# Fused attention and feed-forward kernel: the first two feed-forward groups in an attention PSUM tile, ScalarE ahead of VectorE on the transposes, k's sums by TensorE, and a new order at both ends of batch 1

## The chip, the core and the metric

The kernel runs on one core of one Trainium2 chip. The metric is the device time in microseconds (us) of one execution. Five engines take part, each with its own instruction stream that runs in order: TensorE (PE in the profile, its weight loads PEld), VectorE (DVE), ScalarE (ACT), GpSimd (POOL) and SyncE (SP, which here only issues DMAs). They wait for each other by semaphores.

## What is computed

Two stages, one after the other, over 8 batches of 576 tokens with 8 heads of 64. The attention of a head is the sum of two parts: a *global* one on q, k and v averaged over groups of four tokens (144 positions, repeated four times at the end), and a *local* one in which a token sees only tokens less than four away.

```python
q_d = q.reshape(B, H, Sd, factor, D).mean(axis=3)       # the same for k and v; factor 4
out_up = np.repeat(sm_attn(q_d, k_d, v_d), factor, axis=2)
mask = np.abs(pos[:, None] - pos[None, :]) < factor
attn = softmax(np.where(mask, scale * q @ k.T, -1e9))
x = (out_up + attn @ v), as [B*S, H*D]                   # 4608 x 512
h = x @ w_in                                             # 512 x 2048
g = np.where(h > 0, h, np.exp(np.minimum(h, 0)) - 1)
out = g @ w_out                                          # 2048 x 512
```

## The kernel before

**Attention.** Work goes by pairs of heads: four pairs a batch, named (batch, pair). For each pair the kernel transposes q and k on TensorE into the PSUM tiles `tq` and `tk`, copies them to SBUF as `qt` and `kt`, multiplies them to scores `sc` (six local blocks of 102x96, L362, and the global 72x144 products, L377), takes exponentials on ScalarE (`pex` local, `dex` global), masks the local ones on VectorE (`mex`), sums denominators with matmuls, takes a reciprocal on VectorE, spreads the reciprocals over 64 partitions each (`rcb`), multiplies with v to `lg`, scales `lg` on VectorE to `gn` and `ln`, and adds the two on GpSimd into `xt`, the input of the feed-forward part. The group averages are kept as sums: `kd` for k, the tail of `qt` for q, `vd` for v. There are three forms of the beginning of a pair. Batch 0 uses `early_transposes` and takes the sums of q and k on VectorE (`sums`, L252) from the finished copies. Batch 1 uses `early_transposes` too, but lets TensorE make the sums into columns of the same PSUM tile (12 more matmuls against the constant `EI`), and VectorE copies them out (L295); its `vd` goes through a corner of `tq` and `tk` as well (L281, L285). Batches 2 to 7 use `transposes`.

**Feed-forward.** Nine blocks of 512 tokens. `mm1(t, fc)` makes one of 16 groups of 128 hidden channels: four 128x128 by 128x512 matmuls into a bank `hp` (L592), an exponential on ScalarE (`e`, L608), two VectorE instructions (L609, L612) that finish the activation in `gt`. `mm2(t, i)` is a quarter of an output tile of 128 tokens: four matmuls into `op` (L623); every fourth ends with a copy on ScalarE (`os`) and a DMA on SP. For block 0, groups 0 and 1 are split: `mm1_begin` does the first three of the four matmuls, which need head pairs 0 to 2 only, and `mm1` does the last one (L600) once pair 3's part of `xt` is there.

**PSUM.** There are eight banks. The tag `two` is a ring of two tiles of two banks each; `tq`, `tk`, the two `sc`, the two `rb` of `spread_pe` and `lg` take turns in it, so that each waits until the tile before it in its slot has been read. The other four banks belong in batch 0 to `rb` and `lg` (pool `pse`), and from `swap_pools` on to the tags `hp` and `misc`, two banks each (pool `psm`); `swap_pools` needs batch 0's last reads to be over.

**Order.** The order of all work is written out by hand. Batch 0 is the list `order`, with extras per pair in `early` and `late`; everything after it is put at a time by `at` and sorted. A step that stands at 13.5 comes after `mm1` of group 13. `slots` holds the times of a batch's transposes and scores, `d0` that of the denominators, `o0` those of the outputs, `mm2_at` those of the output quarters. In batch 0 and early in batch 1 matmuls on zeros (`warm`, `keep_busy`, L152) stand where TensorE would have nothing to do.

**Queues.** v of all batches, and q and k from batch 2 on, come through SP as fp32 and are cast on GpSimd (`cast`). q and k of batches 0 and 1 (`load_qk`, two pairs a call but for the first) and the weights `WI`, `WO` (`load_weights`, eight pieces) are issued by GpSimd and cast on the way. So GpSimd's stream mixes DMA issues, casts and the additions into `xt`.

Of the kernel before, what the change touches and what calls it, by code (L numbers as in the profile page):

```python
# [11 lines left out]
AB = mybir.AluOpType  # L12
AF = mybir.ActivationFunctionType
# [85 lines left out]
def kernel(  # L99
# [156 lines left out]
    def early_transposes(b, j):  # L256
# [10 lines left out]
        for t, x16 in ((tq, q16), (tk, k16)):  # L267
# [3 lines left out]
            if b >= NEARLY:  # L271
                for c in range(NB):
# [4 lines left out]
                         skip_group_check=True)  # L277
            if b >= NEARLY:
                g = 0 if t is tq else 1
# [5 lines left out]
                nc.vector.tensor_copy(out=vd[:, g, :], in_=t[0:KG, 0, HB : HB + 128])  # L285
# [6 lines left out]
            if b < NEARLY:  # L292
                sums(y, x)
            else:
                nc.vector.tensor_copy(  # L295
                    out=_free(y[:, 0:1], [[3, 48], [1, 3]]),
                    in_=_free(t[:, 1, HB : HB + 1], [[1, 48], [48, 3]]),
                )
        stT[(b, j)] = (qt, kt, kd, vd)
# [286 lines left out]
    def mm1_begin(t, fc, n):  # L586
# [3 lines left out]
        hp = hps[fc] = bank("misc" if t == 0 and fc < 12 and fc % 4 >= 2 else "hp", "hp")  # L590
        for dc in range(n):
            nc.tensor.matmul(  # L592
                hp[:], WI[:, dc, 128 * fc : 128 * fc + 128], xts[t][:, dc, :],
# [3 lines left out]
    def mm1(t, fc):  # L597
        if t == 0 and fc < 2:
            hp = hps[fc]
            nc.tensor.matmul(  # L600
                hp[:], WI[:, DMC - 1, 128 * fc : 128 * fc + 128], xts[t][:, DMC - 1, :],
                start=False, stop=True,
            )
        else:
# [3 lines left out]
        nc.scalar.activation(out=e[:], in_=hp[:], func=AF.Exp)  # L608
# [4 lines left out]
            out=gts[t][:, fc, :], in0=hp[:], scalar=0.0, op0=AB.max, in1=e[:], op1=AB.add  # L613
# [24 lines left out]
    def at(time, fn, *args):  # L638
# [3 lines left out]
    open_pool("pse")  # L642
    order = [
        (load_consts, 0, 3), (load_qk, 0, (0,)), (load, 0, 0), (load_qk, 0, (1,)), (load_qk, 1),
        (load, 0, 1), (load, 0, 2), (warm, 9), (early_transposes, 0, 0), (load_consts, 3, 4),
        (cast, 0, 0), (load, 0, 3), (warm, 5), (scores, 0, 0), (cast, 0, 1), (load, 1, 0),
    ]
    early = {0: [(cast, 0, 2), (load, 1, 1), (load_weights, 0), (warm, 4)],
             1: [(cast, 0, 3), (load, 1, 2), (load_weights, 1), (load_qk, 2), (load_consts, 4, 5)],
             2: [(load_weights, 2), (load_qk, 3)]}  # L650
    late = {2: [(load_weights, 3), (load_weights, 4)]}
    for j in range(NPAIR):
# [5 lines left out]
        order += [(early_spread, 0, j), (early_outputs, 0, j), *late.get(j, ())]  # L658
    order += [(swap_pools,), (mm1_begin, 0, 0, DMC - 1), (mm1_begin, 0, 1, DMC - 1)]
# [6 lines left out]
    def mm2_at(t, s):  # L666
        if t:
            return 16 * t + 29.75 + s
        return (16, 16.8, 18, 18.4, 19.4, 20.6, 22, 23.4)[s] if s < 8 else 24.75 + 2.5 * (s - 8)

    SLOTS = (0, 1.6, 3.2, 4.8, 9.7, 11.3, 12.9, 14.5)
    for b in range(NEARLY, B):
        base, slots, d0, o0 = 16 * b + 13 - 26.5, SLOTS, 16.1, (22.5, 24.1)
        if b == 1:
            base, slots, d0, o0 = 1.5, [2 * i for i in range(8)], 16.1, (20.2, 21)
# [57 lines left out]
```

## Time and profile before

| | |
|---|---|
| time, median of 3 runs | 381.12 us (380.46 to 381.86) |
| the profiled execution's own time | 383.99 us |
| its span, first to last instruction | 382.2 us |
| TensorE busy with matmuls | 357.0 us, 93% of the span |
| VectorE, ScalarE, GpSimd busy | 257.3, 204.9, 123.7 us |
| mean granted TensorE clock | 0.978 |

The profile is one execution. A line of a timeline has the start in us, the time from the first start to the last end of a merged run of instructions, the engine, the source line, the operation and its tiles, the number of instructions, and in brackets how long the engine had been idle and what ended that. A row of windows has the busy time of each engine in that stretch and the clock that TensorE was granted (PEclk, 1.00 is full). Times of this page are kept apart from the median of runs without a profile; differences are carried over.

### The profile page before, as it was taken

To read this page: it belongs to the slowest core of one execution; us is meant where nothing else is said; L and a number is where in the kernel's file an instruction comes from. 1 tells how busy PE (TensorE), PEld (TensorE's weight loads), DVE (VectorE), ACT (ScalarE), POOL (GpSimd) and SP (SyncE) were. 2 spreads that over 40 slices of the span, in tenths; PEclk is the share of its full clock that TensorE was granted. 3 is DMA by queue.
4 is the path that set the end of the run, shared out by engine and by line. 5 is a ranking of instruction groups with operands and counts; after the bars stand their busy time and mean duration, and the time that the engine had idled before them with its cause. 6 is when DMAs were issued, how large, how long until landed. Compare 5 with 4: busy or idle time off the path is not lost.

```text
span 382.2 us, 8527 instructions
## 1 busy us (share of the span) xinstructions
PE 357.0 (93%) x3342; PEld 186.2 (49%) x3342; DVE 257.3 (67%) x484; ACT 204.9 (54%) x381; POOL 123.7 (32%) x167
## 2 busy tenths in 40 slices
PE   7987887979889998999999999999999999999996
PEld 3553544445544554555455555554554444444442
DVE  2584767757869686977698779787866775655510
ACT  3561666537755766476647664766473334344421
POOL 4376215059306800770078007701700220000000
PEclk9696999989999999999999999999999999999999
DMA  8999999849149908950897099609311300101012
GB/s 136 190 162 199 199 197 193 170 69 197 20 105 217 171 17 188 242 131 10 183 241 146 9 208 233 129 16 201 101 37 58 86 29 30 54 27 55 29 55 82
DMA packets 116549, 46.08 MB, mean 121 GB/s; under 512 B 100508, under 2 KB 111902, under 8 KB 116510
## 3 DMA queue, kind: packets, MB, share of 16 engines
q1 hardware_dynamic: 101114, 33.63, 42.7%
q0 software_dynamic: 7456, 6.55, 11.0%
q10 hardware_dynamic: 7940, 5.36, 6.6%
q8 instruction: 26, 0.43, 0.5%
q14 instruction: 13, 0.11, 0.1%
HBM read 42.21 MB, written 9.88 MB: 136 GB/s over the span
## 4 chain that ended last, share of the span: by engine, by line
PE 67%; DVE 13%; ACT 10%; ACTq 4%; issue 3%; POOL 1%; DMA 1%; DVEq 0%; POOLq 0%
PE op L623 27%; PE hp L592 24%; DVE gt L612 4%; ACTq L483 3%; ACT pex L385 3%; DVE e L609 2%; PE sc L362 2%; ACT e L608 2%; PE lg L528 2%; PE rb L152 2%; ACT dex L391 2%; DVE mex L397 2%; PE tq L329 1%; PE tq L325 1%; PE tk L339 1%
## 5 line engine op out<-in xcount | busy, mean ns | idle before, releaser
L592 PE MATMUL hp<-xt,WI 128*128 128x512 f16 x574 | 147.7, 382 | 5.9 <-DVE gt L612 4.4
L623 PE MATMUL op<-WO,gt 128*128 128x512 f16 x576 | 146.1, 381 | 0.0
L608 ACT ACTIVATE e<-hp 128x512 f16<-128x512 f32 x144 | 85.3, 600 | 100.1 <-PE hp L592 85.7
L612 DVE SCALAR_TENSOR_TENSOR gt<-hp,e 128x512 f16<-128x512 f32 x144 | 99.6, 692 | 5.4
L609 DVE TENSOR_SCALAR e<-e 128x512 f16<-128x512 f16 x144 | 57.8, 402 | 52.3 <-ACT e L608 50.7
L592 PEld LDWEIGHTS <-WI 128*128 128x128 f16 x574 | 53.7, 98 | 69.4 <-issue 9.7
L623 PEld LDWEIGHTS <-gt 128*128 128x128 f16 x576 | 54.2, 98 | 63.3 <-issue 1.4
L558 POOL TENSOR_TENSOR xt<-ln,gn 128x64 f16<-128x64 f16 (+7 forms) x63 | 41.6, 688 | 71.0 <-DVE ln L548 71.0
L239 POOL CAST v<-v 102x768 f16<-102x768 f32 x32 | 29.1, 909 | 107.8 <-DMA v<-in_v_dram 101.4
L385 ACT ACTIVATE pex<-sc 102x576 f16<-102x576 f32 x64 | 41.4, 647 | 18.6 <-PE sc L377 18.4
L397 DVE TENSOR_TENSOR mex<-pex,const 102x1152 f16<-102x1152 f16 x28 | 25.3, 902 | 19.7 <-ACT pex L385 19.3
L629 ACT COPY os<-op 128x512 f32<-128x512 f32 x36 | 21.2, 588 | 21.2 <-PE op L623 21.0
L391 ACT ACTIVATE dex<-sc 72x288 f16<-72x288 f32 x64 | 25.8, 404 | 0.0
L335 ACT CAST qt<-tq 128x720 f16<-128x720 f32 x24 | 18.2, 758 | 14.0 <-PE tq L329 10.4
L239 POOL CAST k<-k 96x768 f16<-96x768 f32 x24 | 22.3, 931 | 3.9 <-PE tq L325 2.3
L362 PE MATMUL sc<-qt,kt 64*102 64x96 f16 x384 | 17.3, 216 | 6.5 <-ACT kt L290 4.2
L362 PEld LDWEIGHTS <-kt 64*102 64x102 f16 x384 | 12.5, 125 | 20.5 <-ACT e L608 8.1
L239 POOL CAST q<-q 96x768 f16<-96x768 f32 x24 | 20.6, 860 | 2.0 <-DMA q<-in_q_dram 1.3
L548 DVE TENSOR_TENSOR ln<-lg,rcb 128x576 f16<-128x576 f32 x28 | 20.9, 748 | 0.0
L528 PE MATMUL lg<-mex,v 102*64 102x96 f16 x384 | 14.3, 215 | 1.6 <-ACT dex L391 1.3
L344 ACT CAST kt<-tk 128x576 f16<-128x576 f32 x24 | 15.6, 649 | 0.0
L528 PEld LDWEIGHTS <-v 102*64 102x64 f16 x384 | 11.2, 114 | 8.2 <-issue 3.9
(76 smaller groups left out, 261.8 us busy)
## 6 DMA issues: line engine op xcount, KB each, us to landing
v<-in_v_dram SPq DMA_DIRECT2D x32, 288.0 KB
out_dram<-os SPq DMA_DIRECT2D x36, 256.0 KB
q<-in_q_dram SPq DMA_DIRECT2D x24, 288.0 KB
k<-in_k_dram SPq DMA_DIRECT2D x24, 288.0 KB
rcb<-rd ACTq DMA_DIRECT2D x12, 288.0 KB
WI<-in_moe_w_in_dram POOLq DMA_DIRECT2D x4, 512.0 KB, 7.4
WO<-in_moe_w_out_dram POOLq DMA_DIRECT2D x4, 512.0 KB, 14.3
v<-in_v_dram SPq DMA_DIRECT2D x62, 9.0 KB
```

What stands on the lines that cost most here:

```text
L239: nc.gpsimd.tensor_copy(out=x if name != "v16" else x[:], in_=t[:].rearrange("p e c d -> p c e d"))
L362: nc.tensor.matmul(sc[e][0:KW, c // 3, QB * (c % 3) : QB * (c % 3) + QB], kt[r, QB * c : QB * c + KW], qt[r, QB * c : QB * c + QB] if run ...
L385: nc.scalar.activation(out=pex[:, e, :].rearrange("p (g u) -> p g u", g=2), in_=sc[e][0:KW, :, 0:HB], func=AF.Exp, scale=SCALE,)
L391: nc.scalar.activation(out=dex[:, e], in_=sc[e][0:KG, :, HB : HB + SD], func=AF.Exp, scale=SCALE / 16 if run else SCALE,)
L397: nc.vector.tensor_tensor(out=mex[:], in0=pex[:], in1=mk2, op=AB.mult)
L528: nc.tensor.matmul(lg[64 * e : 64 * e + 64, c // 3, QB * (c % 3) : QB * (c % 3) + QB], v16[:, c, e, :], mex[:, e, QB * c : QB * c + QB], s ...
L558: add.tensor_tensor(out=xt(t)[:, j, t0 - TBLK * t : t1 - TBLK * t], in0=ln[:, a:z], in1=_rep4(gn[:, a // 4 : z // 4]), op=AB.add,)
L592: nc.tensor.matmul(hp[:], WI[:, dc, 128 * fc : 128 * fc + 128], xts[t][:, dc, :], start=(dc == 0), stop=(dc == DMC - 1),)
L608: nc.scalar.activation(out=e[:], in_=hp[:], func=AF.Exp)
L609: nc.vector.tensor_scalar(out=e[:], in0=e[:], scalar1=1.0, scalar2=-1.0, op0=AB.min, op1=AB.add)
L612: nc.vector.scalar_tensor_tensor(out=gts[t][:, fc, :], in0=hp[:], scalar=0.0, op0=AB.max, in1=e[:], op1=AB.add)
L623: nc.tensor.matmul(op_[:], gts[t][:, fc, 128 * tt : 128 * tt + 128], WO[:, fc, :], start=(fc == 0), stop=(fc == FCN - 1),)
```

## The change

Six things are changed.

1. **ScalarE first.** In batch 1 the VectorE copy of `vd` is moved from ahead of ScalarE's copy of `tq` (`tk`) to behind VectorE's copy of the sums.
2. **k's sums.** In batch 0, k's sums are made as in batch 1: 12 more matmuls a pair into `tk`, and a copy, on ScalarE, of 128x144 to `kd`. VectorE's L252 is left for q alone.
3. **Groups 0 and 1 of block 0** get the two banks of one tile of the ring `two` in place of two `hp` banks, so that they need not wait for `swap_pools`. Group 0's first three matmuls go ahead of pair 3's outputs, group 1's stand right behind them; `swap_pools` comes last. The groups that borrow `misc` banks are now those with `fc % 4 < 2`.
4. **A fill.** Four matmuls on zeros into a tile of `two` stand behind pair 2's outputs; one warm matmul less after pair 1's transposes.
5. **Loads.** The first k load is issued behind v's first load; `load_qk` 1 (pairs 2 and 3 of batch 0) behind the cast of pair 0's v; `load_weights` 4 behind `mm1_begin`.
6. **The order of batch 1 and of block 0's output quarters.** The first transposes of batch 1 come after three groups in place of two. Three output quarters stand ahead of the first transposes of batch 2 in place of one, and the first scores of batch 2 come ahead of `spread_pe`. Ten quarters in place of seven stand ahead of the second transposes of batch 2, and the last six are spread wider.

```diff
@@ early_transposes
-            if b >= NEARLY:
+            reduced = b < NEARLY and t is tq
+            if not reduced:
                 for c in range(NB):
                     col, step = ((0, 48), (0, 96), (48, 48))[c // 2]
                     flip(lambda r: _free(t[r : r + 64, 1, HB + col : HB + col + 1],
                                          [[step, 2], [1, 48]]),
                          x16, a, c, consts["EI"], start=(c == 0), stop=(c == NB - 1),
                          skip_group_check=True)
...
-                nc.vector.tensor_copy(out=vd[:, g, :], in_=t[0:KG, 0, HB : HB + 128])
...
-            if b < NEARLY:
+            if reduced:
                 sums(y, x)
             else:
-                nc.vector.tensor_copy(
+                copy = nc.scalar.copy if b < NEARLY else nc.vector.tensor_copy
+                copy(
                     out=_free(y[:, 0:1], [[3, 48], [1, 3]]),
                     in_=_free(t[:, 1, HB : HB + 1], [[1, 48], [48, 3]]),
                 )
+            if b >= NEARLY:
+                nc.vector.tensor_copy(out=vd[:, g, :], in_=t[0:KG, 0, HB : HB + 128])
@@ mm1_begin
-        hp = hps[fc] = bank("misc" if t == 0 and fc < 12 and fc % 4 >= 2 else "hp", "hp")
+        if t == 0 and fc < 2:
+            if fc == 0:
+                hps["two"] = two("hp")
+            hp = hps[fc] = hps["two"][:, fc, :]
+        else:
+            hp = hps[fc] = bank("misc" if t == 0 and fc < 12 and fc % 4 < 2 else "hp", "hp")[:]
@@ order
+    def fill(n):
+        t = two("fill")
+        keep_busy(lambda i: t[:, i % 2, :], 512, n)
+
     order = [
-        (load_consts, 0, 3), (load_qk, 0, (0,)), (load, 0, 0), (load_qk, 0, (1,)), (load_qk, 1),
-        (load, 0, 1), (load, 0, 2), (warm, 9), (early_transposes, 0, 0), (load_consts, 3, 4),
-        (cast, 0, 0), (load, 0, 3), (warm, 5), (scores, 0, 0), (cast, 0, 1), (load, 1, 0),
+        (load_consts, 0, 3), (load_qk, 0, (0,), "q"), (load, 0, 0), (load_qk, 0, (0,), "k"),
+        (load_qk, 0, (1,)), (load, 0, 1), (load, 0, 2), (warm, 9), (early_transposes, 0, 0),
+        (load_consts, 3, 4), (cast, 0, 0), (load_qk, 1), (load, 0, 3), (warm, 5), (scores, 0, 0),
+        (cast, 0, 1), (load, 1, 0),
     ]
-    early = {0: [(cast, 0, 2), (load, 1, 1), (load_weights, 0), (warm, 4)],
+    early = {0: [(cast, 0, 2), (load, 1, 1), (load_weights, 0), (warm, 3)],
...
-    late = {2: [(load_weights, 3), (load_weights, 4)]}
+    late = {2: [(load_weights, 3), (fill, 4)]}
...
-        order += [(early_spread, 0, j), (early_outputs, 0, j), *late.get(j, ())]
-    order += [(swap_pools,), (mm1_begin, 0, 0, DMC - 1), (mm1_begin, 0, 1, DMC - 1)]
+        order.append((early_spread, 0, j))
+        if j + 1 == NPAIR:
+            order.append((mm1_begin, 0, 0, DMC - 1))
+        order += [(early_outputs, 0, j), *late.get(j, ())]
+    order += [(mm1_begin, 0, 1, DMC - 1), (load_weights, 4), (swap_pools,)]
@@ mm2_at
-        return (16, 16.8, 18, 18.4, 19.4, 20.6, 22, 23.4)[s] if s < 8 else 24.75 + 2.5 * (s - 8)
+        return (15.3, 16, 16.5, 18, 19, 19.5, 20.5, 21.5, 22.5, 23.2)[s] if s < 10 else 24.75 + 3.3 * (s - 10)
@@ batches
         if b == 1:
-            base, slots, d0, o0 = 1.5, [2 * i for i in range(8)], 16.1, (20.2, 21)
+            base, slots, d0, o0 = 2.5, [2 * i for i in range(7)] + [13.3], 15, (19.5, 20.3)
         elif b == 2:
-            slots = [x - base for x in (16.4, 20.8, 23, 25.5, 27, 28.5, 30, 31.5)]
+            slots = [x - base for x in (17, 18.5, 23.5, 25.5, 27, 28.5, 30, 31.5)]
...
         if b == 1:
-            at(19, spread_pe, b, 0)
-            at(20, spread_pe, b, 2)
+            at(20, spread_pe, b, 0)
+            at(21, spread_pe, b, 2)
```

More of the change, by code (lines that the diff above doesn't have):

```diff
@@ L277, in early_transposes @@
                          skip_group_check=True)
+            g = 0 if t is tq else 1
             if b >= NEARLY:
-                g = 0 if t is tq else 1
                 for c in range(3):
@@ L589, in mm1_begin @@
             gts[t] = sb.tile([128, FCN, TBLK], FP16, tag="gt", bufs=2, name="gt")
-        hp = hps[fc] = bank("misc" if t == 0 and fc < 12 and fc % 4 >= 2 else "hp", "hp")
+        if t == 0 and fc < 2:
[4 more added lines that the diff above has]
+            hp = hps[fc] = bank("misc" if t == 0 and fc < 12 and fc % 4 < 2 else "hp", "hp")[:]
         for dc in range(n):
             nc.tensor.matmul(
-                hp[:], WI[:, dc, 128 * fc : 128 * fc + 128], xts[t][:, dc, :],
+                hp, WI[:, dc, 128 * fc : 128 * fc + 128], xts[t][:, dc, :],
                 start=(dc == 0), stop=(dc == DMC - 1),
@@ L600, in mm1 @@
             nc.tensor.matmul(
-                hp[:], WI[:, DMC - 1, 128 * fc : 128 * fc + 128], xts[t][:, DMC - 1, :],
+                hp, WI[:, DMC - 1, 128 * fc : 128 * fc + 128], xts[t][:, DMC - 1, :],
                 start=False, stop=True,
@@ L607, in mm1 @@
         e = sb.tile([128, TBLK], FP16, tag="e", bufs=3, name="e")
-        nc.scalar.activation(out=e[:], in_=hp[:], func=AF.Exp)
+        nc.scalar.activation(out=e[:], in_=hp, func=AF.Exp)
         nc.vector.tensor_scalar(
@@ L612, in mm1 @@
         nc.vector.scalar_tensor_tensor(
-            out=gts[t][:, fc, :], in0=hp[:], scalar=0.0, op0=AB.max, in1=e[:], op1=AB.add
+            out=gts[t][:, fc, :], in0=hp, scalar=0.0, op0=AB.max, in1=e[:], op1=AB.add
         )
```

## The prediction

> **What bounds the kernel now.** I read the page first: busy shares, the 40 slices, the chain.
>
> ```profile
> PE 357.0 (93%) x3342; PEld 186.2 (49%) x3342; DVE 257.3 (67%) x484; ACT 204.9 (54%) x381; POOL 123.7 (32%) x167
> ...
> PE   7987887979889998999999999999999999999996
> ...
> PEclk9696999989999999999999999999999999999999
> ```
>
> TensorE is the bound. From about 115 us on (slice 12) it is all but full, so there little but its own work counts, and an earlier start of feed-forward block 1 moves the end by as much. What can be won lies ahead of that: idle time, and three dips of the clock. Windows of 3.41 us, the step at which this clock changes, show what goes ahead of a dip:
>
> ```profile
> 7.34:10.75 3.41, 1.99 (x43) 1.26 (x41) 1.67 (x3) 2.22 (x6) 0.00 (x0) 1.00 1.26 186
> 17.58:20.99 3.41, 2.82 (x80) 2.23 (x77) 2.26 (x6) 1.94 (x3) 2.72 (x4) 1.00 0.74 98
> 27.82:31.23 3.41, 2.25 (x46) 1.53 (x44) 2.13 (x6) 1.32 (x3) 1.53 (x2) 1.00 1.27 206
> 31.23:34.65 3.42, 2.60 (x27) 1.75 (x24) 1.39 (x3) 0.76 (x1) 1.83 (x4) 0.50 1.23 200
> 34.65:38.06 3.41, 2.96 (x8) 1.02 (x8) 0.99 (x2) 0.00 (x0) 3.02 (x4) 0.50 1.26 188
> ...
> 75.61:79.02 3.41, 2.10 (x47) 1.41 (x47) 1.18 (x3) 2.21 (x6) 0.00 (x0) 1.00 1.31 217
> 79.02:82.43 3.41, 3.41 (x45) 1.82 (x41) 2.08 (x6) 0.00 (x0) 2.25 (x4) 0.50 0.29 39
> ```
>
> The columns are TensorE, its loads, VectorE, ScalarE, GpSimd, clock, DMA share. After 1.99, 2.25 and 2.10 us of TensorE the clock halved, after 2.82 not. Weighting each matmul of the timeline by the rows and columns of the array that it fills, these windows hold 0.31, 0.31, 0.28 and 0.35 of a full one: narrow matmuls count little, and the edge lies near a third.
>
> Then timelines: TensorE's and ScalarE's at the change of stage.
>
> ```profile
> 30.79 1.59 PE L152 MATMUL rb<-Z 128*128 128x360 f16 x6
> ...
> 35.10 2.72 PE L592 MATMUL hp<-xt,WI 128*128 128x512 f16 x6 [1.26 <-DVE ln L548]
> 37.61 0.82 PE L600 MATMUL hp<-xt,WI 128*128 128x512 f16 x2
> ...
> 43.01 0.82 PE L362 MATMUL sc<-qt,kt 64*102 64x96 f16 x12 [1.01 <-ACT kt L290]
> ```
>
> ```profile
> 41.11 0.64 ACT L290 CAST qt<-tq 128x576 f16<-128x576 f32 x1 [1.71 <-DVE vd L285]
> 42.31 0.64 ACT L290 CAST kt<-tk 128x576 f16<-128x576 f32 x1 [0.56 <-DVE vd L285]
> ```
>
> At 35 us TensorE waits for VectorE because the `hp` banks are still batch 0's, and then runs at half clock. In batch 1 ScalarE waits for VectorE's `vd` twice a pair, and TensorE about 1 us a pair behind it. GpSimd's timeline shows what TensorE must not outrun:
>
> ```profile
> 54.98 0.83 POOL L239 CAST v<-v 102x768 f16<-102x768 f32 x1 [9.53 <-DMA v<-in_v_dram]
> ...
> 60.22 0.82 POOL L239 CAST v<-v 102x768 f16<-102x768 f32 x1 [1.00 <-DMA v<-in_v_dram]
> ```
>
> These are v of (1,3) and (2,0): DMA-bound, usable from 55.8 and 61.0.
>
> **The change part by part.** The sum is against the profiled execution (383.99 us, span 382.2).
>
> **A, the start.** Removed: VectorE's sum of k, 4 x 0.74. Added: 12 matmuls a pair (24 take 0.70 in batch 1, 12 take 0.45: 0.25 to 0.3) and a ScalarE copy (L511 of the same size: 0.28), beside other work except in pair 0, whose scores end 0.3 later. In pairs 2 and 3 TensorE waited 0.30 for `kd`: both go. v's first load leaves SP about 0.65 earlier and meets no q and k of pairs 2 and 3, so I estimate its cast at 10.3 to 11.2, not 11.78. The 0.3 delay puts four instead of two full-width warm matmuls into the window 7.34 to 10.75: weight 0.31 to 0.43, so the clock should hold. From L310 (13.00) to the end of pair 0's `ln` took 6.6 at half clock; by the full-clock rows of pair 2 it is 5.2. Against that, q and k of pairs 2 and 3 are now issued behind that cast, 11.1 to 12.5 (0.68 each on GpSimd, ahead of pair 1's cast, which has until 18.9). The first loads landed 3.7 after issue and these two 2.6 apart, so k lands about 17 (16.3 to 19). Its transposes, at 18.51 before, would be wanted at 16.3, and VectorE's `ln` only frees the next step at 17.4: a loss of 0.7. Full clock with that loss gives -2.1, half clock -0.6, full clock without it -2.8, half clock with the latest landing +1.0. I take **-1.4**, between the two likelier.
>
> **B, fill and first groups.** The fill is 4 x 0.216 = 0.86 at 28.56, where TensorE idled 0.62 before L310 (29.19, then 29.42); the next step waits for `ln` until 30.25 in any case, so it costs nothing; without that cover, 0.23. It adds 0.25 to the weight of the window ending at 31.23, 0.56 in all: no dip. Then the six zero matmuls take 0.97 (row of pair 2), the spread follows the reciprocal (30.89 + 1.06) and ends at 32.4, group 0's three matmuls end at 33.05, pair 3's outputs at 33.5; `gn`, `ln` and `xt` took 1.69 and end at 35.2. L600 starts there, not at 37.61: **-2.4**. With the clock still at half: spread 32.97, three matmuls 1.36, outputs 0.86, 1.69: 36.9, so -0.7.
>
> **C, one tile for two groups.** The built program's waits show that group 1's last matmul waits for group 0's `gt`: both banks are one tile. That is 0.25 matmul, 0.61 exponential, 0.30, 0.69 and hops, 2.0 us, with all of TensorE queued behind it; SP and GpSimd go on. From L600 to the second transposes of batch 1: 2.2, three groups (one ahead of the first transposes) and two more, 0.86 each, transposes 1.75, scores 0.88 come to 9.15 against 8.1 (37.61 to 45.72): **+1.05**; without the wait 8.25, +0.15, and not less, since a group stands ahead that did not. Also, `tk` waits for group 1's `gt`, which ends as `tq` does.
> The Trainium skill (PSUM — Partial Sum Buffer, section "PSUM bank collisions raise a hardware error") asks that engines be kept apart by bank and quadrant; the two groups lie in different banks, so by it this wait would not be needed and the sum would be 371.7. The program's wait decides.
>
> **D, ScalarE first.** Score to score took 7.31, 7.41 and 8.02 (43.01, 50.32, 57.73, 65.75). TensorE's work in it: transposes 1.75, four groups 3.46, scores 0.88, 6.1. ScalarE's copies now follow TensorE at once; VectorE's four small copies come in one block of 0.95, and its whole is 0.69 + 4 x 0.93 + 0.95 = 5.4, ScalarE's 4.8. So TensorE bounds it, and I take 6.25. Second transposes to first of batch 2 took 22.03 (45.72 to 67.75). Now: two periods, then transposes 1.75, group 0.86, quarter 0.86, scores 0.88, two quarters 1.73: 18.6, and 0.6 for VectorE rows stretched while GpSimd casts (`mex` 1.41 at 60.25, else 0.76): **-2.8**. Bounds: -3.4, and 0 if VectorE still paces it. A to D put T(2,0), the first transposes of batch 2, at 62.2; its v is there at 61.0, so at most 1.2 more can be had here.
>
> **E, end of batch 1.** From T(2,0), the first group of block 1 was done 18.7 later (86.43). Now, from T(2,0): denominators end at 2.4, the reciprocal (1.97) at 4.4; quarter 3.3, scores 4.0, two quarters 5.8; exponentials free the ring at 5.9; spread 6.45, quarter 7.3, spread 8.0, quarter 8.85, outputs 9.9, quarter 10.75 (at full clock 0.86, before 1.82), outputs 11.8; `gn` and `ln` of pairs 2 and 3 wait for GpSimd's additions (1.3 a pair), 13.9; the last addition 15.35, group done 15.65. That is -3.0; four hand-overs are drawn tight: **-2.6**, bounds -3.4 and -1.0 (only the half-clock quarter).
>
> **F, later.** Between the second transposes and batch 2's denominators stand three quarters, not five: 1.73 less for TensorE, where VectorE is busy 16 of 20 us. **-0.4**; bounds -1.73 (TensorE paces all of it) and +1.0 (the missing filler leaves idle).
>
> Sum: -1.4 - 2.4 + 1.05 - 2.8 - 2.6 - 0.4 = -8.55: 375.4 on the profiled execution. That lies 2.87 above the median of the runs, 381.12; from there 372.6.
>
> **Rivals.**
> - *The clock dips at C's wait.* About 2 us without work follow 0.65 of group 1 and 1.1 of idle before L600; a window that falls there holds about a quarter. One or two windows at half cost 1.7 to 3.4: 374.3 to 376.0. Where the windows fall is luck; by those of this profile it is just avoided. 24%.
> The Trainium skill (TensorE: Matmul & The Clock Gate, section "Part 1: The HAM clock gate") lets the half rate come "after ≥1 idle window (~3.4µs)". The rows above agree on the length, not on idle: 2.25 of 3.41 was busy. By the rule this rival falls away and the sum stays 372.6.
> - *k of pair 2 comes late.* A is +1.0: 375.0. 8%.
> - *ScalarE first does nothing:* VectorE paces batch 1, D is 0, and E only wins the quarter's clock (-1.0): 377.0. For it: VectorE was busy 5.2 of 7 us; against it: 1.6 us a pair of its idle time were waits for ScalarE. 9%.
> - Two of these together end within 0.5%: 6%.
> - *Slower: the clock stays at half through batch 1.* It decides once 8.55 + 1.9 us are lost, some 21 us of half clock in place of full, six windows; all of 35 to 62 would give 385. Against it: from 38.06 on the windows weigh 0.45 to 0.7, and weights of 0.40 at half clock (14.17, 79.02) brought it back. 8%.
>
> **How the numbers follow.** The forecast has 45%. 0.5%, 1.9 us, is about what a measurement of this kernel can tell from no change. Faster: 45 + 24 + 8 + 9 = 86%; same 6%; slower 8%. Low end: 1.2 at D's floor, 0.8 in E, 1.0 in F: 369.6, so 369.5. High end: ScalarE-first failing with half a dip, 378.5; beyond lie 6% + 8% and some 4% below the low end.
>
> **What would show it.** PEclk full from 28 to 38 (B); L600's second matmul about 2 us behind its first (C); score to score near 6.25, ScalarE's L290 waiting for TensorE, not VectorE (D); T(2,0) at 61 to 63 and no half clock near 80 (E). Wrong it would be by a half clock at 35 to 42, TensorE waiting for a `k` DMA near 16, or score to score above 7.

## The result

The changed kernel takes 380.04 us (median of 20 runs, 376.05 to 382.63), the kernel before 382.54 (20 runs, 380.46 to 388.59): a ratio of 0.9917, 95% interval 0.9888 to 0.9946. Two later comparisons on other chips gave 0.9873 (0.9817 to 0.9928) and 0.9921 (0.9889 to 0.9953). So the change wins about 1%, 3 to 5 us, where 8.5 were forecast; 380.04 lies outside the range of 369.5 to 378.5, though the kernel did get faster. All ratios, and all averages of the clock, leave out runs more than 1.5% above the fastest of the same kernel; medians take in every run.

The profiled execution took 380.59 us, its span 378.8. The page, in the rows that were shown of before:

```profile
PE 358.6 (95%) x3393; PEld 187.5 (49%) x3393; DVE 256.1 (68%) x480; ACT 206.4 (54%) x385; POOL 122.6 (32%) x167
...
PE   8896999998889999999999999999998999999996
...
PEclk9699599999999999999999999999999999999999
```

Of the three dips of the clock the last, in the ninth slice, is gone; the second has moved from the fourth to the fifth slice and is deeper. The windows of 3.41 us around both remaining dips, of this profile (columns as before: TensorE, its loads, VectorE, ScalarE, GpSimd, clock, DMA share, GB/s):

```profile
9.80:13.21 3.41, 1.90 (x39) 1.20 (x39) 2.10 (x3) 3.12 (x7) 2.88 (x4) 1.00 0.71 134
13.21:16.62 3.41, 3.38 (x41) 2.27 (x42) 1.55 (x3) 0.76 (x2) 1.58 (x3) 0.50 1.14 178
...
33.69:37.10 3.41, 1.12 (x4) 0.32 (x5) 2.15 (x4) 0.60 (x1) 2.22 (x3) 1.00 1.23 193
37.10:40.52 3.42, 2.06 (x5) 0.55 (x4) 1.97 (x4) 0.60 (x1) 3.05 (x5) 0.50 1.28 199
40.52:43.93 3.41, 3.41 (x56) 2.75 (x56) 1.97 (x5) 1.24 (x3) 0.16 (x1) 0.50 1.22 198
43.93:47.34 3.41, 3.41 (x10) 1.02 (x10) 1.49 (x4) 1.24 (x3) 0.67 (x1) 0.50 1.21 196
```

After 1.12 us of TensorE the clock halves and stays there for three windows. TensorE's timeline of the same stretch says why there was so little work:

```profile
35.57 0.38 PE L608 MATMUL hp<-xt,WI 128*128 128x512 f16 x1 [1.14 <-DVE xt L561]
38.46 0.58 PE L608 MATMUL hp<-xt,WI 128*128 128x512 f16 x1 [2.52 <-DVE gt L620]
38.84 1.91 PE L600 MATMUL hp<-xt,WI 128*128 128x512 f16 x4
...
43.68 3.62 PE L600 MATMUL hp<-xt,WI 128*128 128x512 f16 x8
47.23 0.52 PE L365 MATMUL sc<-qt,kt 64*102 64x96 f16 x12
47.81 1.90 PE L600 MATMUL hp<-xt,WI 128*128 128x512 f16 x8
49.64 0.70 PE L248 MATMUL tq<-const,q 96*64 96x96 f16 x24
...
53.20 0.48 PE L365 MATMUL sc<-qt,kt 64*102 64x96 f16 x12
```

L608, the last matmul of groups 0 and 1, begins at 35.57 (before: 37.61) and then stands 2.9 us apart; eight matmuls that take 1.90 at full clock take 3.62; the second transposes of batch 1 begin at 49.64, where the kernel before had 45.72. Behind that the change does what it should: scores follow each other by 5.97 (47.23 to 53.20; before 7.31), and ScalarE waits for TensorE instead of VectorE:

```profile
42.36 0.64 ACT L290 CAST qt<-tq 128x576 f16<-128x576 f32 x1 [0.91 <-PE tq L282]
43.92 0.64 ACT L290 CAST kt<-tk 128x576 f16<-128x576 f32 x1 [0.93 <-PE tk L282]
```

By the first transposes of batch 2 (67.81, before 67.75) gains and losses are even. The first group of feed-forward block 1 then ends at 83.44, not 86.43, and most of that is kept to the end. The rows from which this is read, of before:

```profile
45.72 0.70 PE L248 MATMUL tq<-const,q 96*64 96x96 f16 x24
...
67.75 0.48 PE L325 MATMUL tq<-const,q 96*128 96x120 f16 x6
...
85.40 1.03 PE L592 MATMUL hp<-xt,WI 128*128 128x512 f16 x4
```

and of after:

```profile
67.81 0.48 PE L328 MATMUL tq<-const,q 96*128 96x120 f16 x6
...
82.21 1.23 PE L600 MATMUL hp<-xt,WI 128*128 128x512 f16 x4
```

### The profile page after: what moved, and what is told of

The parts are those of the page before. It is cut to its first block, busy times and chain, and to the rows that moved or that the text cites. A ratio compares the mean times of both kernels' runs of the same rounds, so it can differ in the third digit from the quotient of the medians.

```text
span 378.8 us, 8635 instructions
## 1 busy us (share of the span) xinstructions
PE 358.6 (95%) x3393; PEld 187.5 (49%) x3393; DVE 256.1 (68%) x480; ACT 206.4 (54%) x385; POOL 122.6 (32%) x167
## 4 chain that ended last, share of the span: by engine, by line
PE 75%; DVE 9%; ACT 6%; ACTq 3%; DMA 2%; issue 2%; POOL 2%; DVEq 0%; POOLq 0%; SPq 0%
PE op L631 28%; PE hp L600 28%; DVE gt L620 3%; PE sc L365 3%; ACTq L486 3%; DVE e L617 2%; ACT e L616 2%; PE lg L531 2%; POOL xt L561 2%; DVE mex L400 1%; PE tk L342 1%; ACT dex L394 1%; DMA k<-in_k_dram 1%; PE tk L248 1%; PE tq L332 1%
## 5 line engine op out<-in xcount | busy, mean ns | idle before, releaser
L600 PE MATMUL hp<-xt,WI 128*128 128x512 f16 x574 | 149.3, 385 | 5.7 <-DVE gt L620 5.3
L617 DVE TENSOR_SCALAR e<-e 128x512 f16<-128x512 f16 x144 | 58.5, 407 | 51.6 <-ACT e L616 49.7
L239 POOL CAST v<-v 102x768 f16<-102x768 f32 x32 | 28.2, 882 | 97.1 <-DMA v<-in_v_dram 96.8
L338 ACT CAST qt<-tq 128x720 f16<-128x720 f32 x24 | 18.2, 758 | 13.1 <-PE tq L332 9.6
L365 PE MATMUL sc<-qt,kt 64*102 64x96 f16 x384 | 16.1, 216 | 1.2 <-ACT kt L347 1.0
L347 ACT CAST kt<-tk 128x576 f16<-128x576 f32 x24 | 15.6, 650 | 0.2 <-PE tk L342 0.2
```

The costliest lines, as they stand in the source:

```text
L239: nc.gpsimd.tensor_copy(out=x if name != "v16" else x[:], in_=t[:].rearrange("p e c d -> p c e d"))
L365: nc.tensor.matmul(sc[e][0:KW, c // 3, QB * (c % 3) : QB * (c % 3) + QB], kt[r, QB * c : QB * c + KW], qt[r, QB * c : QB * c + QB] if run ...
L600: nc.tensor.matmul(hp, WI[:, dc, 128 * fc : 128 * fc + 128], xts[t][:, dc, :], start=(dc == 0), stop=(dc == DMC - 1),)
L617: nc.vector.tensor_scalar(out=e[:], in0=e[:], scalar1=1.0, scalar2=-1.0, op0=AB.min, op1=AB.add)
```

## The experiments

Ratios are to the kernel before on the same chip, with 95% intervals; 0.01 is 3.8 us. The experiments ran on four chips (the first four of them on one), so medians of different experiments compare only roughly. "Group 0's last" is the start of its fourth matmul; T(b,j) are the transposes of pair j of batch b.

**The changed kernel again, and two ways around the wait.**

> The changed kernel once more, as the measure for the three runs beside it. My theory (the wait of group 1 and the clock): TensorE idles 2 to 3 us between the last matmul of group 0 and that of group 1, and the window of 3.41 us that holds this idle time weighs under a third of full work, so the clock halves somewhere between 34 and 48 us in most executions, the second transposes of batch 1 stand near 49.6 and the first of batch 2 near 67.8; time 379 to 381.5. If instead the place of the windows is luck, as my prediction had it, this profile may show the clock full there, the second transposes near 45 and a time near 376.

Ratio 0.9873 (0.9817 to 0.9928). This profile has a span of 373.9, 4.9 shorter, with the same wait:

```profile
32.42:35.83 3.41, 0.38 (x1) 0.10 (x1) 2.17 (x4) 0.60 (x1) 3.12 (x5) 1.00 1.28 192
35.83:39.24 3.41, 3.15 (x29) 1.48 (x28) 1.32 (x4) 1.19 (x2) 2.17 (x3) 0.50 1.23 195
```

```profile
33.40 0.38 PE L608 MATMUL hp<-xt,WI 128*128 128x512 f16 x1 [1.14 <-DVE xt L561]
36.09 0.58 PE L608 MATMUL hp<-xt,WI 128*128 128x512 f16 x1 [2.31 <-DVE gt L620]
```

Here nearly all idle time fell into one window, so only one window at half followed, and the clock held through the start; T(1,1) stands at 44.67, T(2,0) at 63.26. Both theories were half right: the clock dips here too, but how long is luck.

> The last matmuls of groups 0 and 1 are issued together, ahead of both activations, so group 1's no longer waits for group 0's activation. Theory of the wait and the clock: the wait of 2.5 us between them goes, a group follows at once, the window weighs about 0.45 instead of 0.19 and the clock stays full; second transposes of batch 1 at 44.5 to 45.5 instead of 49.6, first transposes of batch 2 at 64 instead of 67.8 (v of that pair is cast by 63.4), time 3.0 to 4.5 below the changed kernel. Rival, the transfers: v of batch 2's first pair and the loads behind it set the pace whatever TensorE does, first transposes of batch 2 stay at 66 to 68 and the time within 1 us of the changed kernel.

```diff
-            hp = hps[fc]
-            nc.tensor.matmul(hp, ... fc ...)
+            for f in (0, 1) if fc == 0 else ():
+                nc.tensor.matmul(hps[f], ... f ...)
+            hp = hps[fc]
```

Ratio 0.9809 (0.9756 to 0.9861). In the profile the two L608 follow each other without a gap (36.32), but the wait is taken up by the next user of the tile, the second half of T(1,0), and the clock dips behind it (42.38 to 45.80):

```profile
37.70 0.70 PE L248 MATMUL tq<-const,q 96*64 96x96 f16 x24
38.34 0.36 PE L282 MATMUL tq<-v,const 102*72 102x128 f16 x3
41.17 0.70 PE L248 MATMUL tk<-const,k 96*64 96x96 f16 x24 [2.48 <-DVE gt L621]
```

So T(1,1) came at 47.81, not at 45, and T(2,0) at 66.11, not at 64. The ratio is better than the changed kernel's, by an unclear margin: it rests on four of six runs, and the median of all six, 377.59, is only 1.2 below that of the changed kernel on this chip.

> The wait stays, but ten matmuls on zeros (10 x 0.216 = 2.2 us) into a free bank stand in it, between the last matmuls of groups 0 and 1. This parts the wait from the clock. If the half clock is what cost, the clock stays full from 34 to 48, the second transposes of batch 1 stand near 46.5 (49.6 less about 3 of half clock) and the time is 2 to 3 us below the changed kernel, some 1 above the run without the wait. If the wait alone costs, it is as the changed kernel within 0.7. If the clock dips for another reason, the dip stays in spite of the zeros.

```diff
+            if fc == 1:
+                zb = bank("misc", "zb")
+                keep_busy(lambda i: zb[:], 512, 10)
```

Ratio 0.987 (0.9837 to 0.9904). In this profile the clock stays full from 4.88 to 373.5 us, with the wait in place:

```profile
34.26 0.38 PE L611 MATMUL hp<-xt,WI 128*128 128x512 f16 x1 [1.14 <-DVE xt L561]
34.47 2.32 PE L152 MATMUL zb<-Z 128*128 128x512 f16 x10
37.15 0.38 PE L611 MATMUL hp<-xt,WI 128*128 128x512 f16 x1 [0.36 <-DVE gt L623]
```

From group 0's last to T(1,1) it takes 10.51 us, against 14.07 and 11.27 in the two profiles above. In the stretch, that parts wait and clock. In time it does not: the median, 378.48, is only 0.3 to 1.6 below those of the changed kernel, not the 2 to 3 expected, and on the same chip the ratios are alike (0.987 and 0.9873). Nor do its other runs keep the clock full: theirs is 0.986 to 0.994, and one window of 3.41 us at half rate makes 0.0045 of a span of 375 us. No profile shows where they lost it.

**The start.**

> The changed kernel, but with the first k load ahead of v's first load, as before the change. In the changed kernel that k landed at 7.31 instead of 5.69 and its transposes began at 7.35 instead of 6.37. If v's load took the queues from it: k lands at 5.7 again, first scores at about 8.2 instead of 9.17, pair 0's outputs up to 1 us earlier; what comes behind waits for k of pairs 2 and 3 (landed 19.03), so pair 3's denominators move from 30.3 to 29.6 to 30.3 and the time by 0 to -0.7. If the late k cost nothing: no difference in time, and pair 3's denominators stay at 30.3. If the whole start moves: -1.0 and denominators at 29.3.

```diff
-        (load_consts, 0, 3), (load_qk, 0, (0,), "q"), (load, 0, 0), (load_qk, 0, (0,), "k"),
+        (load_consts, 0, 3), (load_qk, 0, (0,)), (load, 0, 0),
```

Ratio 0.9935 (0.9896 to 0.9973): no gain, rather a loss, which no expectation had. Its mean clock, 0.980, is the lowest of all the kernels (0.988 for the changed kernel on this chip). In this profile k landed at 6.88, v was cast at 10.49 (9.78 in the run beside it) and the clock came to full only at 9.93, so it can't say what k's place is worth.

> The changed kernel with the start as before: the loads in their old order and k's sums on VectorE. My forecast gave the new start 1.4. The runs so far show the third transposes at 15.5 with the old start and at 16.5 to 16.8 with the new one where the clock stayed full. If the new start only won by the clock of one profile: time within 1 of the changed kernel or up to 1.5 below it, third transposes near 15.5. If the forecast is right: third transposes near 18 and 1 to 2 longer.

```diff
-            reduced = b < NEARLY and t is tq
+            reduced = b < NEARLY
...
-        (load_consts, 0, 3), (load_qk, 0, (0,), "q"), (load, 0, 0), (load_qk, 0, (0,), "k"),
-        (load_qk, 0, (1,)), (load, 0, 1), ..., (cast, 0, 0), (load_qk, 1), ...
+        (load_consts, 0, 3), (load_qk, 0, (0,)), (load, 0, 0), (load_qk, 0, (1,)), (load_qk, 1),
+        (load, 0, 1), ..., (cast, 0, 0), ...
...
-(load_weights, 0), (warm, 3)]
+(load_weights, 0), (warm, 4)]
```

Ratio 0.9906 (0.9873 to 0.994), as the whole change; third transposes at 16.08, group 0's last at 33.68 (33.40 in the better run of the changed kernel). The new start wins nothing that can be measured.

**The shared tile.**

> The changed kernel with groups 0 and 1 in two banks of their own again, begun behind the change of pools as before; all else of the change stays. Theory: the shared tile is the step that lost: group 1's last matmul, and the second half of the first transposes behind it, wait for activations. Without it, from group 0's last matmul to the second transposes of batch 1 it takes 8.0 to 8.6 instead of 11.3, while the groups begin 0.8 to 1 later; first transposes of batch 2 at 60 to 61 (63.3 in the better run of the changed kernel), median 2 to 3.5 below the changed kernel, 375.5 to 377. Rival: the loads of batch 2 hold the first transposes of batch 2 at 63 either way; then within 0.8 of the changed kernel.

```diff
-        if t == 0 and fc < 2:
-            if fc == 0:
-                hps["two"] = two("hp")
-            hp = hps[fc] = hps["two"][:, fc, :]
-        else:
-            hp = hps[fc] = bank("misc" if ... fc % 4 < 2 else "hp", "hp")[:]
+        hp = hps[fc] = bank("misc" if ... fc % 4 >= 2 else "hp", "hp")[:]
...
-        if j + 1 == NPAIR:
-            order.append((mm1_begin, 0, 0, DMC - 1))
...
-    order += [(mm1_begin, 0, 1, DMC - 1), (load_weights, 4), (swap_pools,)]
+    order += [(load_weights, 4), (swap_pools,), (mm1_begin, 0, 0, DMC - 1), (mm1_begin, 0, 1, DMC - 1)]
```

Ratio 0.9853 (0.9811 to 0.9896), median 377.24. No wait, no dip between 19.40 and the end:

```profile
36.02 0.59 PE L603 MATMUL hp<-xt,WI 128*128 128x512 f16 x2
36.46 1.03 PE L595 MATMUL hp<-xt,WI 128*128 128x512 f16 x4
37.41 0.70 PE L248 MATMUL tq<-const,q 96*64 96x96 f16 x24
...
43.48 0.70 PE L248 MATMUL tq<-const,q 96*64 96x96 f16 x24
```

7.46 from group 0's last to T(1,1): a little less than expected, 3.8 to 6.6 less than with the shared tile. The groups did begin later, as expected, and more so in this profile, whose clock was at half from 12.57 to 19.40. T(2,0) came at 62.51, not at 60 to 61, and there TensorE waited 0.95 for v of that pair, which GpSimd cast late because it had landed late. So the rival, the loads, was right in part:

```profile
62.51 0.48 PE L328 MATMUL tq<-const,q 96*128 96x120 f16 x6
63.94 0.49 PE L332 MATMUL tq<-v,const 102*72 102x128 f16 x6 [0.95 <-POOL v L239]
```

The median is 1.5 to 2.8 below those of the three comparisons of the changed kernel. The mean of its 6 runs, 377.0, is 2.0 (0.9 to 3.1) below that of the 35 runs that enter the three ratios of the changed kernel, 379.0, on other chips, and 2.0 (0.7 to 3.2) below that of the kernel with the old start and the shared tile on the same chip.

**ScalarE first and the end of batch 1, taken out and put in alone.**

> The changed kernel with VectorE's copy of vd ahead of ScalarE's copies again, as before the change: only the ScalarE-first step is undone. If ScalarE first is worth what I forecast, score to score in batch 1 goes from 5.9 to 6.4 back to 7.3 to 8.0, the first transposes of batch 2 stand 2.8 to 4 later than in a run of the changed kernel with the same clock, and the time is 2.8 to 4 longer. If it does nothing (the transfers or VectorE pace batch 1), score to score stays below 6.6 and the time within 0.7.

```diff
+                nc.vector.tensor_copy(out=vd[:, g, :], in_=t[0:KG, 0, HB : HB + 128])
             elif j == 0 and t is tq:
...
-            if b >= NEARLY:
-                nc.vector.tensor_copy(out=vd[:, g, :], in_=t[0:KG, 0, HB : HB + 128])
```

Ratio 1.0002 (0.995 to 1.0054), from five of its ten runs: without this step no gain of the change can be measured. Score to score goes back to 7.61, 7.42 and 7.72, and T(2,0) comes at 66.99, 3.7 later than in the run of the changed kernel with the same clock (0.995), within the 2.8 to 4 expected. The old releasers are back, on ScalarE and then on TensorE:

```profile
47.34 0.64 ACT L291 CAST qt<-tq 128x576 f16<-128x576 f32 x1 [2.24 <-DVE vd L286]
48.54 0.64 ACT L291 CAST kt<-tk 128x576 f16<-128x576 f32 x1 [0.57 <-DVE vd L286]
```

```profile
49.24 0.82 PE L364 MATMUL sc<-qt,kt 64*102 64x96 f16 x12 [1.48 <-ACT kt L291]
```

> The kernel before with the ScalarE-first step alone. If the step is worth 2.8 by itself: score to score 6.0 to 6.5 instead of 7.3 to 8.0, first transposes of batch 2 near 63 to 64.5 instead of 67.75 and the time 2.5 to 4 below the kernel before. If it needs the rest of the change (its gain only meets another wait at the end of batch 1): score to score falls, but the first group of block 1 ends no earlier than 85.5 and the time is within 1 of the kernel before. If VectorE or the loads pace batch 1: score to score above 7 and no difference.

```diff
-                nc.vector.tensor_copy(out=vd[:, g, :], in_=t[0:KG, 0, HB : HB + 128])
             elif j == 0 and t is tq:
...
                     in_=_free(t[:, 1, HB : HB + 1], [[1, 48], [48, 3]]),
                 )
+                nc.vector.tensor_copy(out=vd[:, g, :], in_=t[0:KG, 0, HB : HB + 128])
```

The reverse, in the kernel before. Ratio 0.9831 (0.9765 to 0.9896): this step alone gives at least as much as the whole change. Score to score 6.26, 5.93, 5.96. T(2,0) begins at 58.67, not at the 63 to 64.5 expected; 3.4 of that stand ahead of the step, as group 0's last is at 34.25 here and at 37.61 before. It meets the floor that I had named, v of that pair, though at 59.7 and not at 61.0:

```profile
58.67 0.47 PE L325 MATMUL tq<-const,q 96*128 96x120 f16 x6
59.80 0.49 PE L329 MATMUL tq<-v,const 102*72 102x128 f16 x6 [0.65 <-POOL v L239]
```

From T(2,0) to the end of the first group of block 1 it takes 20.6, one window of it at half clock: part of the gain is lost there.

> The changed kernel with the times of batch 1 and of block 0's output quarters as before the change (first transposes of batch 1 after two groups, seven quarters in the old places, scores of batch 2 behind the spread, outputs late). If the new order is worth the 2.6 of the forecast, from the first transposes of batch 2 to the end of the first group of feed-forward block 1 it takes 18.2 to 18.8 instead of 15.5 and the time is 2 to 3.2 longer. If only the half clock near 80 in the profile of before made those 18.7, it takes 17.5 to 17.8 and the time is 1 to 2 longer. If the order does nothing, 15.5 and no difference.

```diff
-        return (15.3, 16, 16.5, 18, 19, 19.5, 20.5, 21.5, 22.5, 23.2)[s] if s < 10 else 24.75 + 3.3 * (s - 10)
+        return (16, 16.8, 18, 18.4, 19.4, 20.6, 22, 23.4)[s] if s < 8 else 24.75 + 2.5 * (s - 8)
...
-            ... = 2.5, [2 * i for i in range(7)] + [13.3], 15, (19.5, 20.3)
+            ... = 1.5, [2 * i for i in range(8)], 16.1, (20.2, 21)
...
-            slots = [x - base for x in (17, 18.5, 23.5, ...
+            slots = [x - base for x in (16.4, 20.8, 23, ...
...
-            at(20, spread_pe, b, 0)
-            at(21, spread_pe, b, 2)
+            at(19, spread_pe, b, 0)
+            at(20, spread_pe, b, 2)
```

Ratio 0.9895 (0.9836 to 0.9955, few runs). From T(2,0) at 63.17 to the end of that group it takes 19.9 in this profile, with the clock at half from 79.71 to 83.12 as before the change; a second dip follows at 89.95. The window at half rate can make at most 1.7 of the 19.9 (half of 3.41); what is left, 18.2, is where the theory that the order is worth 2.6 had it. In time the difference to the whole change isn't measurable.

> The kernel before with the new order of batch 1 and the output quarters alone. If the two steps add up (ScalarE first 0.983, both 0.981 with a median 2.4 lower), this gives 0.988 to 0.996: a gain of 2 to 3 behind the first transposes of batch 2, less what the group and the two quarters ahead of them cost. If the order only pays behind ScalarE first, because batch 1 is paced by VectorE and so the added group and quarters come on top: 0.998 to 1.006, first transposes of batch 2 2 to 3 later than in the profile of before, first group of block 1 at 86 to 87 as before.

The last diff with its signs turned, in the kernel before. Ratio 0.9973 (0.9944 to 1.0003): about 1 us (2.1 less to 0.1 more). T(2,0) moves to 69.24 (before 67.75), by less than expected, and the first group of block 1 ends at 84.87 instead of 86.43: the 3 us come, and half of them pays for the group and the two quarters put ahead, since ScalarE, and TensorE behind it, still wait for VectorE in batch 1 (both profiles also have windows at half clock ahead of T(2,0), this one from 60.76 to 64.17, so the size of the shift is rough):

```profile
43.09 0.82 PE L362 MATMUL sc<-qt,kt 64*102 64x96 f16 x12 [1.45 <-ACT kt L290]
```

> The kernel before with ScalarE first and the new order of batch 1 and the output quarters, without the new start, the shared tile and the fill. ScalarE first alone gave 0.983 of the time before, with 20.6 from the first transposes of batch 2 to the end of the first group of block 1. Theory: the new order takes that to 15.5 to 16 and costs one group and two quarters ahead of it (2.6), so 2 to 3 more are won: ratio 0.974 to 0.978, median 373.5 to 375, below all kernels so far. Rival: the end of batch 1 is held by v of batch 2 and by GpSimd's additions, and the order wins nothing on top: ratio 0.981 to 0.985. Rival: the start is needed as well: between these.

That edit and the one of ScalarE first together, in the kernel before. Ratio 0.9813 (0.9759 to 0.9866), median 375.00. 15.6 from T(2,0) to the end of the group:

```profile
60.82 0.48 PE L325 MATMUL tq<-const,q 96*128 96x120 f16 x6
...
75.22 1.23 PE L592 MATMUL hp<-xt,WI 128*128 128x512 f16 x4
```

Two of the six parts of the change, 7.2 us by the ratio; the whole change has 3 to 5. The median is where the theory had it, the ratio is in the range of the rival that the order wins nothing on top of ScalarE first. The profiles say how both can be: T(2,0) comes 2.15 later than with ScalarE first alone and the first group of block 1 ends 2.8 earlier (76.45 against 79.28, where that profile has its window at half), but a new dip of the clock follows at 106.03. What the order adds in time is not shown. This beats both kernels; the changed kernel with its quiet stretches filled, further down, does as well.

**The clock.**

> The changed kernel with TensorE's three quiet stretches filled: four zero matmuls behind pair 0's scores, five behind the first matmuls of groups 0 and 1 (into a bank of batch 0 that nobody reads any more), the last matmuls of both groups issued together, and the first transposes of batch 1 one group later, so that group 1's activation has time. By the theory that the median of the changed kernel stands above its forecast because the clock halves in its quiet stretches: mean clock 0.995 or more in nearly all runs, times close together at 374.5 to 376.5, a good 3 below the changed kernel's median. If the clock only goes along with another cause (loads that come late), the mean clock rises and the times stay at 378 to 380. If the fill itself delays the work, over 380.

```diff
-..., (warm, 5), (scores, 0, 0),
+..., (warm, 5), (scores, 0, 0), (warm, 4),
...
+    def fill_rb(n):
+        t = early_two("rb")
+        keep_busy(lambda i: t[:, i % 2, :], 512, n)
...
-    order += [(mm1_begin, 0, 1, DMC - 1), (load_weights, 4), ...
+    order += [(mm1_begin, 0, 1, DMC - 1), (fill_rb, 5), (load_weights, 4), ...
...
-            ... = 2.5, [2 * i for i in range(7)] + [13.3], 15, ...
+            ... = 2.5, [1, 2.9, 4.6, 6.7, 8.2, 10, 12, 13.3], 15, ...
```

With the last matmuls issued together, as above. Ratio 0.9778 (0.9728 to 0.9828), median 375.74, mean clock 0.994. The median is as expected, the clock almost: two of the six runs reach 0.995. The profile, of the longest of them, has the wait again at `tk`, a dip from 41.24 to 44.65 and another from 109.51 to 112.92. Since the last matmuls and the order of batch 1 were changed as well, the gain isn't shown to be that of the zeros.

> The best so far (kernel before with ScalarE first and the new order) with its two quiet stretches filled: four zero matmuls behind pair 0's scores and six ahead of the first matmuls of groups 0 and 1, in idle time of 1.03 and 1.54. If half clock is what lifts the median over the best runs: mean clock 0.994 or more in most runs and a median of 372.5 to 374, 1 to 2 below the same kernel without the zeros. If the clock only goes along with other delays: median 374.5 to 376 at whatever clock.

```diff
-..., (warm, 5), (scores, 0, 0), (cast, 0, 1), ...
+..., (warm, 5), (scores, 0, 0), (warm, 4), (cast, 0, 1), ...
...
-    order += [(swap_pools,), ...
+    order += [(fill_rb, 6), (swap_pools,), ...
```

These zeros stand in the kernel with ScalarE first and the new order alone. The mean clock rises from 0.990 to 0.993, the median does not fall: 377.06, ratio 0.9869 (0.9813 to 0.9924), against 375.00 without zeros. The intervals overlap; that zeros pay is not shown. The two profiles show why they had little to win: each has one dip behind its start, the same one (106.03 without zeros, 106.23 with them), and it lies behind both fills.

> The changed kernel once more, beside the two above on one chip: ratio to the kernel before 0.985 to 0.992, mean clock near 0.986 as in the kernel before, and times that fall by about 2.3 for each 0.01 of clock. A ratio below 0.98 would say that the first comparison was unlucky.

Ratio 0.9921 (0.9889 to 0.9953), mean clock 0.987, at the edge of what was expected. Its profile dips from 34.68 to 44.92, three windows.

## Why the prediction was wrong

**The step that failed is C, "one tile for two groups", +1.05.** Against the profile of before, with the mean of the three profiles of the changed kernel (spans 378.8, 373.9, 377.1), step by step:

| stretch | before | after, three profiles | forecast | measured |
|---|---|---|---|---|
| start to group 0's last (A, B) | 37.61 | 35.57, 33.40, 33.43 | -3.8 | -3.5 |
| to T(1,1) (C) | 8.1 | 14.07, 11.27, 13.82 | +1.05 | **+4.95** |
| to T(2,0) (D) | 22.03 | 18.17, 18.59, 19.07 | -2.8 | -3.4 |
| to the first group of block 1 (E) | 18.68 | 15.63, 15.62, 15.62 | -2.6 | -3.05 |
| to T(3,2) (F) | 34.92 | 35.72, 35.76, 35.72 | -0.4 | +0.8 |

The forecast sums to -8.55, the measured column to -4.2. Of the 4.35 between them C makes 3.9 and F 1.2; A and B gave 0.3 less than I said, D and E 1.05 more.

**C.** I had the mechanism, group 1 waiting for group 0's `gt`, and the length of its idle time nearly: 2.0 forecast, 2.3 to 2.5 measured, the longest with VectorE's L617 stretched to 0.99 (else 0.29) while GpSimd casts. Two sizes were wrong. First, I let the wait lengthen the stretch by only 0.9 (9.15 against 8.25). In the three profiles of kernels with own banks for these groups, ScalarE first and the new order, the stretch takes 7.35 to 8.16; with the wait in place, filled, and the clock full it takes 10.51. So the wait costs 2.4 to 3.2. The wait of `tk` for group 1's `gt`, which I put at nothing, is 0.44 of that.

Second, I left the dip out of the sum: I gave it 24% and wrote that where the windows fall is luck. All seven profiles of kernels that keep this wait open dip there: the three above and those with the new start taken back, k ahead of v, `vd` first and the old order (37.10 to 47.34 at the longest, one to three windows). In the three with own banks none does. The dip adds 0.8 to 3.6 to the 10.51. Of the 3.9 that C was off, the wait is 1.4 (10.51 for 9.15) and the dip 2.5 on average. In these profiles luck decided only how long the half rate lasted, and none of the 38 runs of the changed kernel has a mean clock above 0.995, which is one window at half.

I could have seen it: the idle time ahead of L608, one matmul and the wait make 3.8 us (32.26 to 36.09 in the better run), longer than a window, so that some window must hold at least half of it wherever the windows fall. I wrote the pieces down, but priced them at the phase of one profile.

The Trainium skill (TensorE: Matmul & The Clock Gate, section "Part 1: The HAM clock gate") calls the window free-running: it does not start with the kernel. The profiles agree: the first rise to full rate came at 3.93, 6.38, 5.11 and 9.93, which are 0.52, 2.97, 1.70 and 3.11 behind a multiple of 3.41. Its condition for the half rate, a whole idle window, which would have struck out this rival, does not hold here: 1.12, 0.38, 1.39 and 1.21 us of TensorE in a window were followed by half rate, and so were 1.90 of narrow matmuls.

**A and B.** Against the one profile of before, -3.5 looks right. But that profile ran at half clock from 10.75 to 17.58 and from 31.23 to 38.06, four windows ahead of group 0's last; of three other profiles with the old start and banks one has none there, one has one and one has three. Group 0's last came at 37.61, 34.25, 34.49 and 36.35 in four profiles with the old start and banks, mean 35.7, and at 32.65 to 36.32 in seven with the new start and the shared tile, mean 34.1: 1.6 gained, with a spread of 3.7 within the seven. The part of it that is A can't be told from nothing, by the run with the old start (0.9906 against 0.9917, 0.9873 and 0.9921). The step "v's first load leaves SP about 0.65 earlier" came true (cast at 10.33, not 11.78), but I did not price what it runs into: the first k landed at 7.31 instead of 5.69, its transposes began at 7.35 instead of 6.37, and k of pairs 2 and 3 landed at 19.03, the late end of my range (16.75 and 16.59 in the other two profiles, near the 17 that I had taken). The first k came late in those as well, at 7.58 and 7.65; with the old start it landed between 5.69 and 7.01 in six profiles.

So in the profiles B wins 1 to 2 and C loses about 5: the new home of the two groups is a net loss. The times say the same, more mildly: with own banks the changed kernel is 2.0 us faster (0.9 to 3.1). With B's 1 to 2 on top, C cost an estimated 3 to 4 in time, where I had 1.05. D with E and F has 0.9813; the whole change has 0.987 to 0.992. The first half of the change, which I had at -2.75, takes back 2 to 4 us; that is measured across chips, and the intervals leave its size open.

**D** was right, and more: the step by which the change stands or falls (0.9831 alone, 1.0002 for all else without it, from four and five runs). I had 6.25 score to score, the three profiles have 5.9 to 6.8, and the whole stretch, forecast at 19.2, takes 18.2 to 19.1. "ScalarE first does nothing" is refuted.

**E** was right in its own stretch, 15.61 to 15.64 for 15.65 to 16 forecast, in twelve of the thirteen profiles that have it; the one with own banks takes 16.73, with the wait of 0.95 for v. In time it is not shown to pay: alone about 1 us, with an interval that reaches nothing, and on top of D unclear.

**F** came out at its other end. With fewer quarters TensorE waits for activations in front of batch 2's denominators; the profile after has

```profile
99.72 1.02 PE L600 MATMUL hp<-xt,WI 128*128 128x512 f16 x4 [1.62 <-DVE gt L620]
```

where the profile of before waited half as long:

```profile
101.78 1.02 PE L592 MATMUL hp<-xt,WI 128*128 128x512 f16 x4 [0.76 <-DVE gt L612]
```

In the kernel with ScalarE first and the new order alone a new dip of the clock stands at 106.03, behind a window with 1.67 of TensorE; both kernels with filled stretches have it as well (106.23 and 109.51). This is the kind of idle time that I had named, as +1.0, and not chosen.

**The base.** I moved the sum from the profiled execution (383.99) to the median of three runs, 381.12. Over 20 runs that median is 382.54, so 1.4 of the miss of 7.4 are the base. And I booked as gains the half clock of one profile in A, B and E, some 3.5 us (0.8, 1.7 and 1.0), though the changed kernel halves its clock as often: mean clock 0.987 over 35 runs, as over 64 runs of the kernel before. In both, a run is 2.3 to 2.4 us longer for each 0.01 of clock; extended to full clock, the two lines meet it at 375.8 and 380.0. So by this estimate the change is worth 4.2 at equal clock, where the forecast without those 3.5 had 5.05.

**What stays open.** Whether the clock makes all of that 2.3: matmuls at half rate are shown, but zeros that raised the clock went with a shorter time in one kernel, which had other edits too, and not in the two others. Why k ahead of v cost time, and lowered the clock. Behind T(3,2) the three profiles of the changed kernel take 259.3 to 259.6 to the end and that of before 260.9; I have not traced this to a step. Other places for the zeros were not tried.

## What to carry to other kernels

Add up the idle time around a wait before you price it: of a quiet stretch longer than the clock's window, some window holds at least half wherever the windows fall. Here that cost the full rate in seven profiles of seven, and the price was the wait plus one to three windows at half rate. Two accumulators in one tile were tied together by the tile, though their banks differ; taking the wait from one user of the ring only handed it to the next. Measure a bundle of edits by taking each out and putting each in alone: here one of six, ScalarE first, wins at least as much by itself as all six together, and another, the shared tile, gives about 2 us back.

## What the hardware showed that I had not expected

The clock's half rate follows the weight of a window better than its busy time. By my weighting (the rows and columns of the array that a matmul fills, for as long as it takes at full rate, as a share of a full window), the 25 windows of the sixteen profiles behind which the full rate was lost, up to 130 us, weigh 0.06 to 0.35, though TensorE was busy for up to 2.5 us in them. Windows with only 1.8 us busy kept it where they weighed more: every one from 0.36 up did. Between 0.32 and 0.35 both happened, so the weighting is not exact. At half rate, 0.29 (profile after, from 13.21), 0.31 and 0.32 (from 37.10 and 40.52) stayed there though TensorE was up to 100% busy, and 0.41 and 0.45 (from 16.62 and 43.93) brought the full rate back. By this weighting the dip lasted three windows because narrow transposes at half rate (40.52 to 43.93, busy throughout) were not enough to end it.

The wait is one that the program was built with, and it followed the tile, not the bank: in the changed kernel the two groups lie in different banks of one tile and waited 2.3 to 2.5 us; in separate tiles they follow each other at once (36.02). By the rule of the Trainium skill weighed in the prediction (PSUM — Partial Sum Buffer, section "PSUM bank collisions raise a hardware error") this wait is not needed; the run with separate tiles agrees.
